# Means of v by band products, their spreads on GpSimd, and a planner that picks one of two engines

## The chip, the cores and the metric

One core of a Trainium2 chip runs the whole program. The metric is the device time of one execution in microseconds; the median of three runs of the kernel before is 602.4 us (602.11 to 602.69).

## What is computed

The reference is attention with a local window and block summaries, then two dense two-layer networks on the 1536 tokens:

```python
B, H, S, D = 2, 8, 768, 64; block, window = 32, 16
k_sum = k.reshape(B, H, S // 32, 32, D).max(axis=3)
v_sum = v.reshape(B, H, S // 32, 32, D).mean(axis=3)
scores_l = where(|i - j| < 16, q @ k.T / 8, -1e9)          # local
scores_s = q @ k_sum.T / 8 + log(32)                       # 24 summaries
a = softmax(concat([scores_l, scores_s]))
x = (a @ concat([v, v_sum])).reshape(1536, 512)
h = x @ w_in;   x = (max(h, 0) + alpha * min(h, 0)) @ w_out     # 512 -> 2048 -> 512
h = x @ w_in2;  y = (h * sigmoid(h)) @ w_out2
```

## The kernel before

Heads go in pairs (4 a batch), queries in 6 blocks of 256 tokens (3 a batch). A pair's keys lie in SBUF as windows of 24 summaries and 160 keys, its values (tile vs, 120 partitions by 12 windows by 128) as 24 means and 96 neighbours; the even windows have the means in partitions 0 to 23, the odd ones in 96 to 119. A group (one block of one pair) passes through these steps: scores (line 554, PE), mask and maximum (L566, L577, DVE), exponentials (L584, ACT), sum and reciprocal (L593, L594, DVE), normalisation (L600, GpSimd), transposes (L606, PE), their copy to pT (L611, ACT), the values (L622, PE), and x as a high and a low half in the rounded float32 format that PE takes fast (L633 ACT, L637 DVE). The four pairs of batch 0 come first, two blocks of each, then the rest, block by block.

The 24 means of a pair are made thus: vT (the whole v of the pair, transposed, 384 KB) is loaded by `load_vt`, for batch 0 into the first half of y, which is free until then, for batch 1 into a staging buffer; DVE sums each block (`sum_v`, L524); PE transposes the sums into PSUM (`turn_v`, L529); ACT writes them with the factor 1/32 from PSUM into all windows of vs (`spread`, L535, step s0 for the first two windows of each kind, s1 for the other four). The maxima of k are made by DVE (L499) and copied to the other five windows by DVE (`copy_k`, L508).

A matrix product of the networks is three products of halves (`three`, L288 to L290). A weight arrives in 512 KB pieces (`load_next`, L121), is put together by three DVE operations on its bits (L147, L151, L154), rounded by ACT (L160, high) and subtracted by GpSimd or DVE (L163, low). The first three pieces land in y beside vT, the later ones in two staging buffers (`raw`). In the first network's first pass each block goes through products with w_in, an activation in four steps (L342 ACT, L348 DVE, L354 ACT, L357: the low half gl, on GpSimd for these blocks), then products with w_out, whose pairs of banks DVE copies to y (L378).

The order of all this, up to two items past the attention, is not written out: every step has an engine, a cost in us, the steps it must follow, a due time (key) and the buffers that it takes and gives. `plan` (L845) repeats: on each engine, of the first 60 steps in order of due time, those whose predecessors are planned; of these the one that can start first; of all engines the earliest. GpSimd's steps and those DVE steps that are marked with lock do not overlap in the plan. Where PE has a gap in the plan, `fill` (L458) puts small products on zeros (L460), up to FILL_END. Loads all go through SP's queue (step `load`, with a modelled wire of RATE MB/us). The instructions are then issued in the plan's order, and the hardware runs each engine's in that order. After it come the remaining passes from a written list.

Of the kernel before, what the change touches and what calls it, by code (L numbers as in the profile page):

```python
# [18 lines left out]
SUB = 64  # L19
PAD = WINDOW  # L20
WIN = SUB + 2 * PAD
P = 128
# [3 lines left out]
AT_KEYS, AT_SUMS, AT_MEANS, AT_SPREAD = -1.1, 1.64, 2.2, 2.35  # L26
AT_EXPS, AT_NORM, AT_TURN, AT_VALUES = 0.22, 0.3, 1.83, 3.2
AT_IN = 5.3
AT_LATER, ITEM_STEP = 4.14, 0.8
CONV, CONV_STEP = -2.94, 0.88  # L30
CONV2, CONV2_STEP = 14.11, -0.2
BATCH, BATCH_STEP = 6.61, 3.24
NQ = 6
STAGE = 2
AT_SC, AT_MASK, AT_X, AT_ACT, AT_OUT = -0.21, 0.0, 3.3, -0.0, 1.54
# [7 lines left out]
def tile_blocks_attention_mlps(  # L43
# [24 lines left out]
    QB = 256  # L68
    BPB = S // QB
# [19 lines left out]
    y_v = y.rearrange("p a n -> p (a n)")[:, :NPAIR * S].rearrange("p (a n) -> p a n", n=S)  # L89
    y_w = y.rearrange("p a n -> p (a n)")[:, NPAIR * S:].rearrange("p (a n w) -> p a n w", n=512, w=2)  # L90
# [34 lines left out]
    def conv_next(eng):  # L125
# [36 lines left out]
        def low():  # L162
# [155 lines left out]
    def activation(u, i, ni, banks):  # L318
# [37 lines left out]
        def four():  # L356
            (nc.gpsimd if early else nc.vector).tensor_tensor(out=gl, in0=g, in1=gh, op=ALU.subtract)  # L357
# [5 lines left out]
    gpool, ps_o = [], []  # L363

    def out_pair(u, m):

        _, ch, t0, n, _ = u
        ps = ps_mm.tile([P, 512], F32, tag="mm", name="ps").rearrange("p (m n) -> p m n", m=2)
        for j in range(2):
            c = slice((m + j) * P, (m + j + 1) * P)  # L370
            for i in range(CF):
                hi, lo = pieces[0, ch, 1, i]
                three(ps[:, j], (hi[:, c], lo[:, c]), g_t[t0, ch * CF + i, 0], i == 0, i == CF - 1)

        def follow():
            if m == KT - 2 and t0 + n == NTOK:
                through[0] = passes.index((0, ch))
            nc.vector.tensor_copy(out=y[:, m:m + 2, t0:t0 + n], in_=ps)  # L378

        return follow  # L380
# [59 lines left out]
    def convert(eng):  # L440
        r = conv_next(eng)
        if r is not None:
            pending.extend(r)
            load_next()

    NG = NBLK * NPAIR
    with ExitStack() as scope0:
# [14 lines left out]
        cst = kv.tile([P, P + 4 * NC], F32, name="cst", bufs=1)  # L462
        ident = cst[:, 0:P]
        mask = cst[:, P:]
# [12 lines left out]
        def load_vt(b, p):  # L477
            if b == 0:
                t = y_v[:, p]
            else:  # L480
                t = stage.tile([P, 512, 2], F32, name="raw").rearrange("p n w -> p (n w)")[:, :S]
# [24 lines left out]
        def copy_k(b, p):  # L506
            t = kt_t[b, p]
            nc.vector.tensor_copy(  # L508
                out=t[:, 1:, :NB], in_=t[:, 0:1, :NB].to_broadcast([P, NTWO, NB])
            )  # L510

        vr_t, pv_t = {}, {}

        def halve_v(b, p):
            v = vt_t[b, p].rearrange("p (n i) -> p n i", i=BLOCK)
            for w in (BLOCK // 2, BLOCK // 4):
                nc.gpsimd.tensor_tensor(
                    out=v[:, :, :w], in0=v[:, :, :w], in1=v[:, :, w:2 * w], op=ALU.add
                )
# [7 lines left out]
        def turn_v(b, p):  # L527
            pt = ps_mm.tile([P, 512], F32, tag="mm", name="pv")
            nc.tensor.transpose(pt[:NB, :P], vr_t.pop((b, p)), ident)  # L529
            pv_t[b, p] = pt  # L530

        def spread(b, p, s0, s1):
            t, ps = vs_t[b, p], pv_t[b, p]
            for at in (t[:NB, s0:s1], t[WIN:, NTWO + s0:NTWO + s1]):
# [4 lines left out]
                    scale=1.0 / BLOCK,  # L539
# [57 lines left out]
        def normalize(blk, p):  # L597
            e = e_t[blk, p]
            rs = sums.pop((blk, p))
            nc.gpsimd.tensor_tensor(out=e, in0=e, in1=rs.to_broadcast([P, 4, NC]), op=ALU.mult)  # L600
# [8 lines left out]
        def turned(blk, p):  # L609
            t = att.tile([NC, 512], F32, tag="pT", name="pT")  # L610
            nc.scalar.copy(out=t, in_=pt_t.pop((blk, p))[:NC])  # L611
            pT_t[blk, p] = t

        def values(blk, p):
# [3 lines left out]
            for i in range(2):  # L618
                for s in range(2):
                    for h in range(2):  # L620
                        c = (2 * h + i) * P + s * SUB
                        nc.tensor.matmul(  # L622
                            ps[h * D:(h + 1) * D, i * P + s * SUB:i * P + (s + 1) * SUB],
                            s_[:, s * NTWO + 2 * j + i, h * D:(h + 1) * D],
                            t[:, c:c + SUB],
                            start=True,
                            stop=True,
# [57 lines left out]
        steps = []  # L685

        def step(name, engine, cost, after, key, f, *a, take=(), give=(), lock=False, size=0):
            steps.append((key, len(steps), name, engine, cost, after, f, a, take, give, lock, size))

        def load(name, key, f, *a, size, after=(), take=()):  # L690
# [3 lines left out]
                "raw": STAGE, "w": 2, "g": 1, "gh": 3}  # L694
# [3 lines left out]
        for p in range(NPAIR):  # L698
            load(("k", 0, p), -100 + at, load_k, 0, p, size=0.41, take=["k"])
            load(("q", 0, p), -100 + at + 0.1, load_q, 0, p, size=0.13, take=["q"])  # L700
            if p == 0:
                load("cst", -100 + at + 0.2, lambda: nc.sync.dma_start(out=cst, in_=consts), size=0.31)
            load(("vt", 0, p), -100 + at + 0.3, load_vt, 0, p, size=0.39)
# [9 lines left out]
        for k, (blk, p) in enumerate(order):  # L713
# [3 lines left out]
            if b and j == 0:  # L717
# [3 lines left out]
                load(("vt", b, p), t + 1.5, load_vt, b, p, size=0.39, take=["raw"])  # L721

        for b in range(B):
            for p in range(NPAIR):
                k = where[b * BPB, p]
                step(("km", b, p), "DVE", 0.87, [("k", b, p)], k + AT_KEYS, prep_k, b, p)
                step(("K", b, p), "DVE", 0.22, [("km", b, p)], k + AT_KEYS, copy_k, b, p, lock=True)
                step(("vr", b, p), "DVE", 0.87, [("vt", b, p)], k + AT_SUMS, sum_v, b, p, BLOCK,
                     take=["vr"], give=["raw"] * (b > 0))

                step(("pv", b, p), "PE", 0.12, [("vr", b, p), "cst"], k + AT_MEANS, turn_v, b, p,
                     take=["mm"], give=["vr"])
# [4 lines left out]
        for k, (blk, p) in enumerate(order):  # L737
# [11 lines left out]
            step(("e", *g), "POOL", 0.95, [("rs", *g)], k + AT_NORM, normalize, *g, lock=True)  # L749
# [4 lines left out]
            step(("o", *g), "PE", 0.47, [("pT", *g), (f"s{int(j > 0)}", b, p)], k + AT_VALUES, values, *g,  # L754
# [6 lines left out]
        def bits(n):  # L761
            halves[n] = conv_next(nc.gpsimd)

        for n in range(3 * CF):
# [4 lines left out]
            step(("lo", n), "POOL", 1.24, [("hi", n)], t + 0.02, lambda n: halves[n][1](), n,  # L769
                 give=["w"], lock=True)  # L770
# [29 lines left out]
        for blk in range(NBLK):  # L800
# [10 lines left out]
            for i in range(0, CF, 2):  # L811
# [3 lines left out]
                else:  # L815
# [6 lines left out]
                step(("a3", blk, i), "POOL", 1.24, [("a2", blk, i)], t0 + AT_ACT, act, blk, i, 3,  # L822
                     give=["g"], lock=True)
            for m in range(0, KT, 2):
# [4 lines left out]
                step(("oc", blk, m), "DVE", 0.6, [("op", blk, m)] + [("vr", 0, p) for p in range(NPAIR)]  # L829
                     + [("cv", n) for n in range(y_w.shape[1])], t,  # L830
                     lambda blk, m: follows[blk, m](), blk, m, give=["mm"])
# [13 lines left out]
        def plan():  # L845
# [4 lines left out]
            locked, wire, out = 0.0, 0.0, []  # L850
            kind, gaps, until = "ps", [], 0.7
# [6 lines left out]
            while any(left.values()):  # L858
                best = None
                for e, todo in left.items():  # L860
                    found = []
                    for s in todo[:60]:
# [5 lines left out]
                        at = max([free[e], *(end[x] for x in after)])  # L868
                        for r in take:
                            at = max(at, sorted(hold[r])[take.count(r) - 1])  # L870
                        if lock:
                            at = max(at, locked)
# [10 lines left out]
                left[e].remove(s)  # L883
# [60 lines left out]
def _layout(q, k, v, moe_w_in, moe_w_out, moe_alpha, moe2_w_in, moe2_w_out):  # L944
# [31 lines left out]
    for t, first in enumerate((0, P, S - P)):  # L976
# [5 lines left out]
        m[t, SUB:, :WIN] = np.where(ok, 0.0, -1000000000.0)[SUB:]  # L982
    consts = np.concatenate(
        [np.eye(P, dtype=np.float32)] + [m[t] for t in (0, 1, 1, 2)], axis=1
# [31 lines left out]
```

## Time and profile before

| | |
|---|---|
| median of 3 runs | 602.4 us |
| the profiled execution | 601.8 us, its span 600.0 us |
| PE busy | 584.0 us (97%) |
| DVE, ACT, GpSimd busy | 415.9, 256.4, 56.1 us |
| granted TensorE clock, mean | 0.994 of full |
| HBM read, written | 48.82, 3.15 MB |

Busy times are of one execution. A product's end is modelled, and the fillers count as busy, so PE's share says little where fillers run; the windows below tell the stages apart. The attention and the first pass lie in the first 155 us or so.

### The profile page before, as it was taken

Reading aid. Unit: us, or ns where it says so; the run is one execution under the profiler, and the core shown is the slowest. Engines: PE = TensorE matmul, PEld = TensorE weight load, DVE = VectorE, ACT = ScalarE, POOL = GpSimd, SP = SyncE. Lnnn points to the kernel's source line nnn. Section 1 sums busy time; section 2 is a strip of 40 time slices with the busy share of each in tenths; the row PEclk is TensorE's granted clock in tenths of the full one; section 3 lists DMA queues with packets and bytes.
Section 4 is the critical chain, followed back from the end, with each engine's and each line's share of the span. In section 5 each row is a group of like instructions: output and inputs, shape, how many; then the busy total and the mean of one; then the engine's idle time right before and its main releaser. Section 6 shows DMA issues by size and latency. Waiting matters only on the chain.

```text
span 600.0 us, 9132 instructions
## 1 busy us (share of the span) xinstructions
PE 584.0 (97%) x3575; PEld 490.1 (82%) x3575; DVE 415.9 (69%) x752; ACT 256.4 (43%) x584; POOL 56.1 (9%) x53
## 2 busy tenths in 40 slices
PE   7989989999899999999999999999999999999997
PEld 5767879899788888888888888888888888888886
DVE  4799888538895573438896789875962598856322
ACT  4888766634242421322543546544612164215110
POOL 0245545321100000000000000000000000000000
PEclk8999989999999999999999999999999999999999
DMA  8988743002542040004030003141130042200111
GB/s 256 314 269 243 208 160 109 32 1 71 153 129 70 3 138 1 0 1 129 19 105 29 0 8 133 71 157 54 37 105 0 1 140 71 72 1 1 69 72 70
DMA packets 24091, 52.55 MB, mean 88 GB/s; under 512 B 2288, under 2 KB 11760, under 8 KB 24048
## 3 DMA queue, kind: packets, MB, share of 16 engines
q1 hardware_dynamic: 24048, 51.97, 27.7%
q8 instruction: 28, 0.46, 0.3%
q14 instruction: 15, 0.12, 0.1%
HBM read 48.82 MB, written 3.15 MB: 87 GB/s over the span
## 4 chain that ended last, share of the span: by engine, by line
PE 78%; DMA 8%; issue 5%; DVE 5%; POOL 2%; SPq 1%; ACT 0%; POOLq 0%; DVEq 0%
PE ps L289 26%; PE ps L288 26%; PE ps L290 25%; DMA raw<-in_w 3%; DMA y<-in_w 1%; DMA q<-in_qT 1%; DMA kT<-in_kT 1%; DVE w L151 1%; DVE w L154 1%; POOL gl L357 1%; DVE w L147 1%; DMA raw<-in_vT 1%; PE sc L554 1%; PE pt L606 1%; PE o L622 1%
## 5 line engine op out<-in xcount | busy, mean ns | idle before, releaser
L288 PE MATMUL ps<-xh,wl 128*128 128x512 f32 (+1 forms) x352 | 127.9, 363 | 0.4 <-POOL wl L163 0.3
L290 PE MATMUL ps<-xh,wh 128*128 128x512 f32 (+1 forms) x352 | 126.8, 360 | 0.0
L289 PE MATMUL ps<-xl,wh 128*128 128x512 f32 (+1 forms) x352 | 126.7, 360 | 0.0
L289 PE MATMUL ps<-gl,wh 128*128 128x512 f32 (+1 forms) x240 | 83.5, 350 | 1.9 <-POOL gl L357 1.8
L290 PE MATMUL ps<-gh,wh 128*128 128x512 f32 (+1 forms) x240 | 83.2, 349 | 0.0
L288 PE MATMUL ps<-gh,wl 128*128 128x512 f32 (+1 forms) x240 | 81.3, 352 | 0.3
L357 DVE TENSOR_TENSOR gl<-g,gh 128x512 fp32r<-128x512 f32 x84 | 57.6, 688 | 31.4 <-ACT gh L354 31.3
L288 PEld LDWEIGHTS ps<-xh,wl 128*128 128x128 f32 x352 | 66.4, 189 | 11.0 <-POOL wl L163 0.8
L289 PE MATMUL ps<-wl,gh 128*128 128x512 f32 (+1 forms) x196 | 75.4, 385 | 0.0
L290 PE MATMUL ps<-wh,gh 128*128 128x512 f32 (+1 forms) x196 | 74.9, 385 | 0.0
L288 PE MATMUL ps<-wh,gl 128*128 128x512 f32 (+1 forms) x196 | 74.9, 385 | 0.0
L290 PEld LDWEIGHTS ps<-xh,wh 128*128 128x128 f32 x352 | 66.4, 189 | 10.0
L289 PEld LDWEIGHTS ps<-xl,wh 128*128 128x128 f32 x352 | 66.5, 189 | 9.8
L354 ACT CAST gh<-g 128x512 fp32r<-128x512 f32 x96 | 59.3, 621 | 25.5 <-DVE g L348 22.1
L342 ACT ACTIVATE m<-ps 128x512 f32<-128x512 f32 x48 | 28.6, 597 | 90.5 <-PE ps L290 90.5
L160 ACT CAST wh<-w 128x512 fp32r<-128x512 f32 x64 | 39.5, 620 | 53.3 <-DVE w L154 34.4
L414 DVE TENSOR_TENSOR y<-ps,y 128x512 f32<-128x512 f32 x48 | 32.4, 688 | 41.9 <-PE ps L290 41.7
L348 DVE SCALAR_TENSOR_TENSOR g<-m,nal,ps 128x512 f32<-128x512 f32 (+1 forms) x60 | 37.2, 637 | 22.6 <-ACT m L342 22.5
L289 PEld LDWEIGHTS ps<-gl,wh 128*128 128x128 f32 x240 | 46.1, 192 | 8.0 <-POOL gl L357 2.3
L288 PEld LDWEIGHTS ps<-gh,wl 128*128 128x128 f32 x240 | 46.1, 192 | 6.8 <-POOL wl L163 0.3
L290 PEld LDWEIGHTS ps<-gh,wh 128*128 128x128 f32 x240 | 46.2, 192 | 5.6
L584 ACT ACTIVATE e<-t,nm 128x120 f32<-128x120 f32 x96 | 36.8, 385 | 19.1 <-DVE nm L577 18.5
(83 smaller groups left out, 844.5 us busy)
## 6 DMA issues: line engine op xcount, KB each, us to landing
raw<-in_w SPq DMA_DIRECT2D x61, 512.0 KB, 3.6
vs<-in_vw SPq DMA_DIRECT2D x16, 288.0 KB, 6.8
kT<-in_kT SPq DMA_DIRECT2D x8, 480.0 KB, 5.8
q<-in_qT SPq DMA_DIRECT2D x24, 128.0 KB, 4.9
out<-y SPq DMA_DIRECT2D x11, 256.0 KB, 2.0
y<-in_vT SPq DMA_DIRECT2D x4, 384.0 KB, 7.8
y<-in_w SPq DMA_DIRECT2D x3, 512.0 KB, 7.9
raw<-in_vT SPq DMA_DIRECT2D x4, 384.0 KB, 4.4
```

What stands on the lines that cost most here:

```text
L147: nc.vector.tensor_scalar(out=w, in0=high, scalar1=3, scalar2=0x3FFFFFFF, op0=ALU.logical_shift_left, op1=ALU.bitwise_and,)
L151: nc.vector.scalar_tensor_tensor(out=w, in0=high, scalar=0xC0000000, in1=w, op0=ALU.bitwise_and, op1=ALU.bitwise_or)
L160: nc.scalar.copy(out=hi, in_=w)
L288: i = nc.tensor.matmul(ps, all_, bh, start=first, stop=False, skip_group_check=again)
L289: nc.tensor.matmul(ps, ah, bl, start=False, stop=False, skip_group_check=again)
L290: nc.tensor.matmul(ps, ah, bh, start=False, stop=last, skip_group_check=again)
L342: nc.scalar.activation(out=m[:, j * w:(j + 1) * w], in_=ps, func=AF.Relu, scale=-1.0)
L348: nc.vector.scalar_tensor_tensor(out=g[:, at], in0=m[:, at], scalar=nal[:, f + j:f + j + 1], in1=ps[:, j * n % w:j * n % w + n], op0=ALU.m ...
L354: nc.scalar.copy(out=gh, in_=g)
L357: (nc.gpsimd if early else nc.vector).tensor_tensor(out=gl, in0=g, in1=gh, op=ALU.subtract)
L414: nc.vector.tensor_tensor(out=at, in0=src, in1=at, op=ALU.add)
L584: nc.scalar.activation(out=e[:, u, :], in_=t[:, u, :], func=AF.Exp, bias=nm[:, u:u + 1], accum_out=sm[:, u, 0:1],)
```

## The change

Batch 0's means are products of the loaded windows with a constant band (1/32 where a row of the window belongs to a block): 12 products of 24 columns, accumulated in PSUM, in place of one transpose. So batch 0's vT is not loaded and not summed, all of y's six places take weights, and the rows of vs that the means will fill are zeroed by GpSimd ahead. For both batches ACT copies the means once from PSUM to a small tile (mn), and GpSimd or ACT spreads them from there. A step may be given several engines: each is a candidate, and one is put aside where another would end it over BIAS = 0.68 us sooner. With the values given, K's copies go to ACT or GpSimd (DVE no longer), the spreads to GpSimd or ACT, the normalisation stays on GpSimd, pT goes to ACT or DVE, a weight's low half to GpSimd or DVE, the copy to y to DVE or ACT, gl to GpSimd or DVE, and for block 5 to DVE alone. The due times and the wire's rate are new. The parts for `split` are unused, since it is empty.

```diff
-AT_KEYS, AT_SUMS, AT_MEANS, AT_SPREAD = -1.1, 1.64, 2.2, 2.35
+AT_KEYS, AT_SUMS, AT_MEANS, AT_SPREAD = -2.12, 1.55, 1.71, 4.61
...
-W_FIRST, W_STEP, W_AHEAD = -98.6, 0.28, 3.41
-SLACK, RATE = 0.0, 0.33
-FILL_LESS, FILL_SLOW, FILL_END = 0.19, 4.0, 61.17
-AHEAD, AT_NEXT = 2, 0.0
+W_FIRST, W_STEP, W_AHEAD = -98.67, -1.13, 4.28
+SLACK, RATE = 0.0, 0.28
+FILL_LESS, FILL_SLOW, FILL_END = 0.65, 4.0, 85.65
+K_ON, SP_ON, E_ON, T_ON, L_ON, O_ON = 1, 2, 1, 2, 0, 0
+BIAS = 0.68
+AHEAD, AT_NEXT = 2, 3.58
...
+    quick = (5,)
+    pooled = (0, 1)
+    banded, split, zeroed = (0,), (), (0,)
...
-    y_v = y.rearrange("p a n -> p (a n)")[:, :NPAIR * S].rearrange("p (a n) -> p a n", n=S)
-    y_w = y.rearrange("p a n -> p (a n)")[:, NPAIR * S:].rearrange("p (a n w) -> p a n w", n=512, w=2)
+    y_w = y.rearrange("p a n -> p (a n)").rearrange("p (a n w) -> p a n w", n=512, w=2)
...
+    def copy(eng, out, in_):
+        (eng.copy if eng is nc.scalar else eng.tensor_copy)(out=out, in_=in_)
...
+        NBAND = 2 * NB - 4
+        cst = kv.tile([P, P + 4 * NC + 2 * NBAND], F32, name="cst", bufs=1)
...
+        band = cst[:, P + 4 * NC:].rearrange("p (o c) -> p o c", o=2)
...
             vs_t[b, p] = t
+            if b in zeroed:
+                nc.gpsimd.memset(t[:NB, :NTWO], 0.0)
...
         def turn_v(b, p):
             pt = ps_mm.tile([P, 512], F32, tag="mm", name="pv")
-            nc.tensor.transpose(pt[:NB, :P], vr_t.pop((b, p)), ident)
             pv_t[b, p] = pt
+            if b not in banded:
+                nc.tensor.transpose(pt[:NB, :P], vr_t.pop((b, p)), ident)
+                return
+            t = vs_t[b, p]
+            for n in range(NSUB):
+                odd, m = divmod(n, NTWO)
+                rows, at = (WIN if odd else NC), NB - 4 - 4 * m
+                nc.tensor.matmul(
+                    pt[:NB, :P], band[:rows, odd, at:at + NB], t[:rows, n],
+                    start=n == 0, stop=n == NSUB - 1,
+                )
...
+        def mean_copy(b, p):
+            mn_t[b, p] = t = kv.tile([NB, P], F32, tag="mn", name="mn", bufs=2)
+            nc.scalar.activation(
+                out=t, in_=pv_t[b, p][:NB, 0:P], func=AF.Copy, scale=1.0 if b in banded else 1.0 / BLOCK
+            )
+
+        def pool_spread(b, p, s0, s1, eng):
+            t, m = vs_t[b, p], mn_t[b, p]
+            for at in (t[:NB, s0:s1], t[WIN:, NTWO + s0:NTWO + s1]):
+                copy(eng, at, m.unsqueeze(1).to_broadcast([NB, s1 - s0, P]))
...
-                step(("K", b, p), "DVE", 0.22, [("km", b, p)], k + AT_KEYS, copy_k, b, p, lock=True)
+                step(("K", b, p), (("DVE", 0.22, True), ("ACT", 0.2, False), ("POOL", 0.2, True))[K_ON:K_ON + 2], 0, [("km", b, p)], k + AT_KEYS, copy_k, b, p)
...
+                if b in banded:
+                    step(("pv", b, p), "PE", 2.65, [("v", b, p), "cst"], k + AT_MEANS, turn_v, b, p, take=["mm"])
...
+                if b in pooled:
+                    step(("mn", b, p), "ACT", 0.2, [("pv", b, p)], k + AT_MEANS + 0.1, mean_copy, b, p, take=["mn"], give=["mm"])
+                    step(("s0", b, p), (("POOL", 0.6, True), ("ACT", 0.7, False))[:SP_ON], 0, [("mn", b, p), ("v", b, p)], k + AT_MEANS + 0.1, pool_spread, b, p, 0, QB // P)
+                    step(("s1", b, p), (("POOL", 1.0, True), ("ACT", 1.2, False))[:SP_ON], 0, [("s0", b, p)], k + AT_SPREAD, pool_spread, b, p, QB // P, NTWO, give=["mn"])
+                    continue
...
-            step(("pT", *g), "ACT", 0.5, [("pt", *g)], k + AT_TURN, turned, *g,
+            step(("pT", *g), (("ACT", 0.5, False), ("DVE", 0.6, False))[:T_ON], 0, [("pt", *g)], k + AT_TURN, turned, *g,
...
-            step(("lo", n), "POOL", 1.24, [("hi", n)], t + 0.02, lambda n: halves[n][1](), n,
-                 give=["w"], lock=True)
+            step(("lo", n), (("POOL", 1.24, True), ("DVE", 0.6, True))[L_ON:], 0, [("hi", n)], t + 0.02, lambda n, eng: halves[n][1](eng), n,
+                 give=["w"])
...
-                step(("a3", blk, i), "POOL", 1.24, [("a2", blk, i)], t0 + AT_ACT, act, blk, i, 3,
-                     give=["g"], lock=True)
+                step(("a3", blk, i), (("POOL", 1.24, True), ("DVE", 0.6, True))[int(blk in quick):], 0, [("a2", blk, i)], t0 + AT_ACT,
+                     lambda blk, i, eng: acts[blk, i][3](eng), blk, i, give=["g"])
...
-                step(("oc", blk, m), "DVE", 0.6, [("op", blk, m)] + [("vr", 0, p) for p in range(NPAIR)]
+                step(("oc", blk, m), (("DVE", 0.6, False), ("ACT", 0.5, False))[O_ON:O_ON + 2], 0, [("op", blk, m)]
...
+                        at = max(free[e], ready)
+                        if any(
+                            max(free[o], ready) + c + BIAS < at + cost for o, c in other.get(s[1], ()) if o != e
+                        ):
+                            continue
```

## Rows read from the trace of the kernel before

**Rows 1.** Windows: start:end, length, busy us (instructions) by engine, clock, DMA share, GB/s

```profile
5.40:36.00 30.60, 26.10 (x328) 20.18 (x328) 23.61 (x53) 21.83 (x80) 8.56 (x9) 0.94 1.03 302
36.00:79.00 43.00, 40.80 (x514) 34.90 (x512) 38.35 (x85) 35.54 (x120) 20.08 (x18) 1.00 0.78 238
79.00:85.00 6.00, 3.13 (x50) 2.34 (x50) 5.90 (x7) 2.17 (x6) 4.65 (x4) 1.00 0.39 115
85.00:90.00 5.00, 5.00 (x52) 4.77 (x53) 4.28 (x10) 4.94 (x17) 1.60 (x2) 0.66 0.43 134
90.00:150.00 60.00, 59.91 (x629) 55.55 (x628) 39.33 (x82) 31.49 (x97) 18.86 (x17) 1.00 0.17 53
150.00:156.00 6.00, 4.02 (x24) 3.31 (x23) 4.54 (x9) 1.86 (x3) 2.15 (x1) 1.00 0.42 124
156.00:597.00 441.00, 440.96 (x1974) 366.25 (x1972) 298.36 (x504) 157.24 (x265) 0.00 (x0) 1.00 0.19 60
```

**Rows 2.** The same windows for line 460 (fillers) alone: PE, PEld, clock, DMA

```profile
5.40:36.00 30.60, 12.59 (x85) 8.81 (x85) 0.94 1.03 302
36.00:79.00 43.00, 6.16 (x41) 3.68 (x41) 1.00 0.78 238
```

**Rows 3.** Chain of waits in time, up to 100 us: start, us, what

```profile
4.45 7.38 DMA kT<-in_kT
...
11.84 8.64 DMA q<-in_qT
...
20.50 8.96 DMA y<-in_w
...
38.18 4.88 DMA raw<-in_w
...
64.70 6.32 DMA raw<-in_w
```

**Rows 4.** Waits: engine line <- releaser: us in total, times, longest

```profile
PE pv L529 <- DVE y L378: 2.6, 1, 2.6
...
PE ps L289 <- POOL gl L357: 1.8, 1, 1.8
```

**Rows 5.** Timeline of DVE and POOL: start, us, engine, line, operation, tiles

```profile
80.38 1.64 DVE L151 SCALAR_TENSOR_TENSOR w<-raw,w 128x512 uint32<-128x512 uint32 x1
...
81.44 1.71 POOL L357 TENSOR_TENSOR gl<-g,gh 128x512 fp32r<-128x512 f32 x1
...
152.85 2.15 POOL L357 TENSOR_TENSOR gl<-g,gh 128x512 fp32r<-128x512 f32 x1 [4.03 <-ACT gh L354]
```

**Rows 6.** Lines by form: operation, shapes xcount | busy us, mean ns | idle before

```profile
L151 DVE SCALAR_TENSOR_TENSOR w<-raw,w 128x512 uint32<-128x512 uint32 x61 | 42.6, 707 | 0.5
...
L524 DVE TENSOR_REDUCE vr<-y 128x24 f32<-128x768 f32 x4 | 3.8, 947 | 0.7 <-DMA y<-in_vT 0.7
...
L508 DVE COPY kT<-kT 128x144 f32<-128x144 f32 x8 | 2.8, 354 | 0.0
...
L357 DVE TENSOR_TENSOR gl<-g,gh 128x512 fp32r<-128x512 f32 x84 | 57.6, 688 | 31.4 <-ACT gh L354 31.3
...
L622 PE MATMUL o<-pT,vs 120*64 120x64 f32 x384 | 15.7, 227 | 0.7 <-DVE xl L637 0.4 <-ACT pT L611 0.3
...
L529 PE MATMUL pv<-cst,vr 128*24 128x128 f32 x8 | 2.2, 277 | 4.5 <-DVE y L378 2.6 <-DVE vr L524 1.1 <-DVE xl L637 0.7
...
L535 ACT ACTIVATE vs<-pv 24x256 f32<-24x256 f32 x16 | 5.9, 370 | 0.4 <-PE pv L529 0.3
...
L535 ACT ACTIVATE vs<-pv 24x512 f32<-24x512 f32 x16 | 9.3, 584 | 0.1
...
L600 POOL TENSOR_TENSOR e<-e,rs 128x480 f32<-128x480 f32 x24 | 23.7, 989 | 58.6 <-DVE rs L594 45.7 <-ACT wh L160 6.5 <-DVE kT L508 2.6
...
L163 POOL TENSOR_TENSOR wl<-w,wh 128x512 fp32r<-128x512 f32 x12 | 16.0, 1334 | 12.1 <-ACT wh L160 12.1
```

**Rows 7.** DMA issues of the page: xcount, KB each, us to landing

```profile
y<-in_vT SPq DMA_DIRECT2D x4, 384.0 KB, 7.8
```

More of the change, by code (lines that the diff above doesn't have):

```diff
@@ L160, in high, with low @@
             nc.scalar.copy(out=hi, in_=w)
-        def low():
+        def low(eng=nc.vector):
             eng.tensor_tensor(out=lo, in0=w, in1=hi, op=ALU.subtract)
@@ L621, in values @@
                         c = (2 * h + i) * P + s * SUB
+                        rows = WIN if s and b in split else NC
                         nc.tensor.matmul(
                             ps[h * D:(h + 1) * D, i * P + s * SUB:i * P + (s + 1) * SUB],
[L624 to L627, printed above, removed]
+                            s_[:rows, s * NTWO + 2 * j + i, h * D:(h + 1) * D],
+                            t[:rows, c:c + SUB],
+                            start=(i, s) == (0, 0) or b not in split,
+                            stop=b not in split,
+                            skip_group_check=b in split,
+                        )
+            if b in split:
+                e_ = t.rearrange("k (h i s c) -> k h s i c", h=2, i=2, s=2)
+                x_ = ps.rearrange("d (i s c) -> d s i c", i=2, s=2)
+                for s in range(2):
+                    for h in range(2):
+                        nc.tensor.matmul(
+                            x_[h * D:(h + 1) * D, s],
+                            mt_t[b, p][:, s, h * D:(h + 1) * D],
+                            e_[:, h, s],
+                            start=False,
+                            stop=s == 1,
+                            skip_group_check=True,
                         )
@@ L683, in tile_blocks_attention_mlps @@
         where = {g: k for k, g in enumerate(order)}
-        steps = []
+        steps, names = [], []
+        engines = {"DVE": nc.vector, "ACT": nc.scalar, "POOL": nc.gpsimd}
         def step(name, engine, cost, after, key, f, *a, take=(), give=(), lock=False, size=0):
-            steps.append((key, len(steps), name, engine, cost, after, f, a, take, give, lock, size))
+            n = len(names)
+            names.append(name)
+            if isinstance(engine, str):
+                steps.append((key, n, name, engine, cost, after, f, a, take, give, lock, size))
+                return
+            for e, cost, lock in engine:
+                steps.append((key, n, name, e, cost, after, f, (*a, engines[e]), take, give, lock, size))
         def load(name, key, f, *a, size, after=(), take=()):
@@ L720, in tile_blocks_attention_mlps @@
                 load(("v", b, p), t + 1.5, load_v, b, p, size=0.6, take=["v"])
-                load(("vt", b, p), t + 1.5, load_vt, b, p, size=0.39, take=["raw"])
+                if b not in banded:
+                    load(("vt", b, p), t + 1.5, load_vt, b, p, size=0.39, take=["raw"])
         for b in range(B):
@@ L850, in plan @@
             locked, wire, out = 0.0, 0.0, []
+            other = {}
+            for s in steps:
+                other.setdefault(s[1], []).append((s[3], s[4]))
+            other = {n: o for n, o in other.items() if len(o) > 1}
             kind, gaps, until = "ps", [], 0.7
@@ L982, in _layout @@
         m[t, SUB:, :WIN] = np.where(ok, 0.0, -1000000000.0)[SUB:]
+    bands = np.zeros((P, 2, 2 * nb - 4), np.float32)
+    for odd, row in ((0, nb + pad), (1, pad)):
+        for i in range(SUB // BLOCK):
+            at = nb - 4 + 2 * odd + i
+            bands[row + i * BLOCK:row + (i + 1) * BLOCK, odd, at] = 1.0 / BLOCK
     consts = np.concatenate(
-        [np.eye(P, dtype=np.float32)] + [m[t] for t in (0, 1, 1, 2)], axis=1
+        [np.eye(P, dtype=np.float32)] + [m[t] for t in (0, 1, 1, 2)] + [bands.reshape(P, -1)], axis=1
     )
```

107 lines of the change are left out of this document (58 added, 49 removed).

## The prediction, made before the changed kernel was run

> **What bounds the kernel now.** I read the windows first, because the share of busy time is a mean over unlike stages. From 156 us to 597 us TensorE is busy 440.96 of 441 us, and from 90 to 150 us 59.91 of 60 [rows 1]: nothing there can be saved except by fewer matmuls, and the change takes none of them away. What can move lies ahead of 90 us and around 152 us. Between 5.4 and 36 us PE shows 26.10 us busy, but 12.59 of that are the filler products of line 460 on zeros, which only keep the clock up [rows 1, 2]; real work is 13.5 us of 30.6. In the same stretch the DMA share is 1.03 at 302 GB/s. Between 36 and 79 us fillers take 6.16 us and PE is idle for another 2.2 us [rows 1, 2]; DVE is busy 38.35 of 43 us. From 79 to 85 us PE works only 3.13 of 6 us, and in the 5 us after it the granted clock is 0.66, the mean of a time at 2.4 GHz and one at 1.2 [rows 1]. At 150 to 156 us PE works 4.02 of 6.
>
> Then the chain of waits says what ends last there. Its early part is one landing after another: 4.45, 11.84 and 20.50 us, each of 7 to 9 us, for kT, q and a weight [rows 3]; the reader sees that no engine but the load queue sets the pace until 29 us. Later pieces of the chain are weights into the two staging buffers (38.18 and 64.70 us) [rows 3]. The two large holes have their releasers in the table of waits: the transpose of batch 1's means waited 2.6 us for a PSUM bank that DVE's copy to y held, and a second matmul waited 1.8 us for GpSimd's low half gl [rows 4]. The timeline shows why the first was late: DVE's conversion beside GpSimd's subtraction took 1.64 us where its mean is 0.707, and GpSimd's own 1.71 us [rows 5, 6].
>
> **The change, part by part.** The sum is made against the profiled execution, 601.8 us (span 600.0 and 1.8 around it); the median of the runs is 602.4, so 0.6 is added at the end. About 0.2% (1.2 us) is what a measurement of this kernel can tell from no change.
>
> A. Four loads of vT, 384 KB each [rows 7], leave the early queue: 1.57 MB at 302 GB/s [rows 1] is 5.2 us; the constants grow by 88 columns (45 KB), 0.15 us back. The last pair's k stands behind three of the four (3.9 us), its v behind all (5.0 net). The chain there is landings, so the gain is real as far as the engines follow. DVE has room for it: it loses four reductions of 0.947 and four copies of 0.354 of 23.61 us [rows 1, 6], so 18.4 us remain for some 25.6. I take -4.0 us; bounds -5.0 and 0. The order of the loads is also rewritten by new keys; a weight more ahead of the last pair is 512 KB, 1.7 us against this.
>
> B. The hole at 79 to 90 us: 2.9 us idle and 5 x (1 - 0.66) = 1.7 us of clock [rows 1]. The copy to y may now go to ACT, which is busy 2.17 of those 6 us [rows 1], and K's copies leave DVE altogether. But the planner's costs know no slow conversion, and GpSimd gets more work that could slow others. What is late next is the conversion itself. I take half, -2.3 us; bounds -4.6 and 0.
>
> C. Block 5's gl goes to DVE alone: 2.15 us there on GpSimd [rows 5] against 0.688 as DVE's mean [rows 6], 1.46 saved on a path where PE waited 1.8 [rows 4]. DVE is busy 4.54 of 6 us [rows 1], so it may stand in a queue: -1.4 us, bounds -1.8 and 0.
>
> D. PE gains 48 band products and loses four transposes. The trace has no matmul of that shape. The values of line 622, with 64 columns on half of the array's width, take 227 ns each with their latency, but overlap: 15.7 us over 384 of them are 41 ns [rows 6]. For 128 columns, if two of them ran beside one another, that is 164 ns, so 2.0 us a pair. The ends: 41 ns (0.5 us a pair) and the transpose's 277 ns with its latency (3.3 us a pair) [rows 6]. I take 2.0, 7.9 us in all, the row that it is nearest to. It lies in place of fillers: 12.59 us of them up to 36 us [rows 2]. Uncovered is what stands in order ahead of a ready product: half of one pair's, +1.0 us; bounds 0 and +7.9, the whole, if the cover is gone. The Trainium skill, FP8 and Floating Point Precision, TensorE Precision Notes, says that true fp32 goes through the array in four passes; 4 x 128 columns at 2.4 GHz would be 213 ns, an estimate, 2.6 us a pair, and the sum by it would be about 0.3 us longer.
>
> E. The spreads: ACT loses two of 0.370 and two of 0.584, 1.91 us a pair [rows 6], and takes a mean's copy (under 0.370) and perhaps K's. GpSimd takes the copies: 1536 elements a pair, at line 600's 0.989 us for 480 not over 3.2 us, and from below near nothing; batch 0 adds a fill with zeros of 768 elements, not over 1.6. ACT stands on no piece of the chain shown [rows 3], so what it gives back is 0; GpSimd is busy 8.56 of 30.6 and 20.08 of 43 us [rows 1], which covers the copies, at 0; without that cover see the second rival. The first values of a pair wait for the second spread, as they did.
>
> F. Three more weights land in y instead of two staging buffers, so fewer wait for a buffer; the two chain pieces were 4.88 and 6.32 us [rows 3], but the wire was 78% busy then [rows 1]. Up to 8.4 us (6.16 + 2.2) stand free on PE there [rows 1, 2]; DVE is 89% busy and sets the next limit. -1.0 us; bounds -4 and +2. K's copies and pT on either engine: 0, under 0.6 us each, PE has fillers beside them.
>
> Sum: 601.8 - 4.0 - 2.3 - 1.4 + 1.0 - 1.0 = 594.1, with 0.6 for the median 594.7 us.
>
> **The rivals.** *First, DVE takes over the pace.* Loads come earlier, but the groups pass at DVE's speed. For it: 89% in the second stretch. Against it: five us of its work leave. Then A and F give nothing and half of B stays: 602.4 - 1.4 - 2.3 + 1.0 = 599.7.
>
> *Second, slower: GpSimd becomes the bound of a batch-0 pair.* Place: between the means and the values. A pair has two normalisations (0.989), a low half (1.334), and now up to 3.2 of copies and 1.6 of zeros: 8.1 us [rows 6]; with the conversion, which the planner locks against GpSimd at 1.65 us, 9.8. A pair takes 30.6 / 4 = 7.65 us now. It decides once copies and zeros cost over 4.3 us a pair, or 2.7 where the lock counts in full. Price 4 x (8.1 or 9.8 - 7.65) = 1.8 or 8.6 us, the middle 5.2. With C and D's uncovered work kept the time is 602.4 + 5.2 - 1.4 + 1.0 = 607.2 (603.8 and 610.6 at the ends). For it: DVE and GpSimd slowed each other at 80 us [rows 5]. Against it: the planner may give spreads to ACT. The Trainium skill, GPSIMD Engine Reference, Specifications, says that GpSimd shares its SBUF interfaces with VectorE, with contention where DVE has two SBUF inputs; the rows at 80 us agree, 1.64 against 0.707. Its section on engine selection calls one-input work on GpSimd roughly line-rate, which at its 1.2 GHz would make the copies 1.3 us a pair, an estimate; no row here shows a copy on GpSimd, and by it this rival would not decide.
>
> *Third, more than forecast.* All of A, B and C, and 4 us of F: 602.4 - 5.0 - 4.6 - 1.8 - 4 = 587.0.
>
> *Fourth, nothing.* The loads keep their place behind weights, the hole moves elsewhere, gains and the band products cancel: 602.
>
> **How the numbers follow.** Forecast 0.52, first rival 0.17, second 0.16, third 0.10, fourth 0.05. Faster: 0.52 + 0.17 + 0.10 = 0.79; same 0.05; slower 0.16. The range runs from 587.0, the third case, to 604.0, the small end of the second; some 0.13 of the second and 0.04 of the third lie outside. The bounds of the forecast's own terms with the same signs lie within it, except where all of D is uncovered, which the second rival's upper part takes in.
>
> **What would show it.** A: the last of batch 0's kT and vs land 4 to 5 us earlier, and the chain's early landings are shorter; wrong if the share of DMA stays at 1 as long as before. B: no PE hole over 1 us near 75 to 90 us, no granted clock under 1 there. C: gl of the last block on DVE, PE busy near 5.4 of 6 us around it. D: 48 products near 2 us a pair, fewer fillers ahead of 36 us. E: GpSimd's copies under 0.5 us for 256 and 1 us for 512 elements, and no values waiting for them. F: weights' landings off the chain. The prediction is wrong if PE's full stretch starts no earlier than now, or if GpSimd or DVE stands between the means and the values.

## The result, and the profile after

The changed kernel takes 596.73 us, the median of four runs (595.28 to 597.33), beside 602.55 for the kernel before: a ratio (of the means) of 0.9895 [0.987, 0.9921], that is 6.3 us less, with 4.8 to 7.8 as the interval; the medians differ by 5.8. The forecast was 594.7 us in a range of 587 to 604. The profiled execution took 596.82 us, its span 595.0.

The same windows as in [rows 1], and the 5 us after 31 us by themselves behind the first row (columns as there):

```profile
5.40:36.00 30.60, 26.97 (x337) 21.40 (x337) 19.95 (x44) 19.86 (x73) 11.50 (x15) 0.94 0.91 257
...
31.00:36.00 5.00, 5.00 (x66) 3.54 (x65) 2.18 (x6) 3.31 (x10) 3.11 (x4) 0.77 0.30 113
36.00:79.00 43.00, 39.26 (x561) 33.06 (x561) 41.81 (x94) 37.73 (x142) 23.70 (x25) 1.00 0.73 219
79.00:85.00 6.00, 5.33 (x74) 4.60 (x71) 5.86 (x13) 3.25 (x12) 2.88 (x3) 1.00 0.37 79
85.00:90.00 5.00, 5.00 (x65) 4.49 (x64) 4.21 (x10) 4.93 (x21) 3.19 (x4) 1.00 0.49 197
90.00:150.00 60.00, 59.44 (x553) 55.78 (x550) 45.11 (x88) 30.27 (x74) 10.75 (x10) 1.00 0.23 80
150.00:156.00 6.00, 6.00 (x48) 5.78 (x47) 3.38 (x7) 2.40 (x4) 0.00 (x0) 1.00 0.61 178
```

Both holes are gone. From 79 to 85 us PE is busy 5.33 of 6 us (before 3.13), and the 5 us after it have the full clock (before 0.66); from 150 to 156 us it is busy 6.00 of 6 (before 4.02). These three rows account for 2.2 + 1.7 + 2.0 = 5.9 us; the two profiled executions differ by 5.0, so they hold the whole gain, and the rest together shows none. The stretch up to 79 us looks as long as it was, and DVE is now nearly full in its second part: 41.81 of 43 us, before 38.35.

What became of the fillers is in the windows of their line alone, and of the band products' line (L536) alone (PE, PEld, clock, DMA):

```profile
5.40:36.00 30.60, 1.99 (x15) 1.20 (x14) 0.94 0.91 257
36.00:79.00 43.00, 2.62 (x16) 1.16 (x16) 1.00 0.73 219
...
5.40:36.00 30.60, 12.42 (x96) 10.17 (x96) 0.94 0.91 257
```

Ahead of 36 us the fillers fell from 12.59 us [rows 2] to 1.99, and the band products took 12.42 in their place. Other work of PE did not come sooner there: without fillers and band products it is 12.56 us, before 13.51. Up to 79 us it is 49.2, before 48.2, about 1 us more. The chain of waits, the table of waits, the timeline (DVE, then PE) around 28 us and the time to landing of the last pair's v say why:

```profile
2.11 4.60 DMA cst<-in_consts
6.73 8.49 DMA vs<-in_vw
15.24 10.43 DMA y<-in_w
...
28.52 4.04 PE pv L536 x24
...
39.16 4.13 DMA kT<-in_kT
```
```profile
PE pv L536 <- DVE xl L685: 2.5, 1, 2.5
...
PE pt L639 <- POOL e L633: 1.6, 3, 1.0
...
PE o L656 <- ACT vs L370: 0.3, 1, 0.3
```
```profile
25.69 0.43 DVE L151 TENSOR_SCALAR w<-y 128x512 uint32<-128x512 uint32 x1 [1.37 <-DMA y<-in_w]
26.15 0.69 DVE L155 SCALAR_TENSOR_TENSOR w<-y,w 128x512 uint32<-128x512 uint32 x1
26.88 0.69 DVE L158 SCALAR_TENSOR_TENSOR w<-y,w 128x512 uint32<-128x512 uint32 x1
...
28.05 0.41 DVE L685 TENSOR_TENSOR xl<-o,xh 128x256 fp32r<-128x256 f32 x1
...
23.18 2.80 PE L536 MATMUL pv<-vs,cst 120*24 120x128 f32 x24
28.52 4.04 PE L536 MATMUL pv<-vs,cst 120*24 120x128 f32 x24 [2.53 <-DVE xl L685]
```
```profile
DMA to landing us min/median/max: 9.7/9.8/9.8
```

Landings still set the chain up to 25.7 us. Then DVE, which had stood 1.37 us for a weight, converts it (three operations), and only behind them makes the low half xl that gives a PSUM bank back; for that bank the last pair's band products waited 2.5 us. Not all of this is the bank's: the last pair's two loads of v, issued at 17.10 and 17.69 us, landed only at 26.8 and 27.5, so the products could have begun 1.7 us sooner at best. They then took 4.04 us where the pair before took 2.80, the clock having fallen (0.77 from 31 to 36 us), and stand on the chain, not under a filler.

The maxima of k of the last pair start as its kT lands (issued at 17.02 us and landed 8.7 us later before, 14.25 and 8.8 after). That pair of batch 0 starts its maximum at 25.75 us before and 23.09 after, and its second load of v is issued at 23.25 before and 17.69 after (the timelines of DVE and of SP; before, then after):

```profile
25.75 0.95 DVE L499 TENSOR_REDUCE kT<-kT 128x24 f32<-128x768 f32 x1
...
23.25 0.33 SPq L489 DMA_DIRECT2D vs<-in_vw  x1
```
```profile
23.09 0.95 DVE L507 TENSOR_REDUCE kT<-kT 128x24 f32<-128x768 f32 x1 [0.97 <-DMA kT<-in_kT]
...
17.69 0.33 SPq L497 DMA_DIRECT2D vs<-in_vw  x1
```

Issued 5.6 us sooner, that load landed 4.3 us sooner, at 27.5 in place of 31.8. These are single traces. In the six traces whose loads keep the changed order (the change and five experiments below) the last kT landed at 22.7 to 24.9 us, in the four with the old order at 25.7 to 26.8; the means lie 2.3 us apart, those of the last v 3.4.

The new operations, in the lines by form, and the line of all GpSimd's spreads (ns: least, median, most):

```profile
L536 PE MATMUL pv<-vs,cst 96*24 96x128 f32 x48 | 7.1, 308 | 0.0
...
L370 POOL COPY vs<-mn 24x512 f32<-24x512 f32 x8 | 6.0, 754 | 0.8 <-ACT mn L556 0.6
L536 PE MATMUL pv<-vs,cst 120*24 120x128 f32 x48 | 5.9, 274 | 2.9 <-DVE xl L685 2.5 <-DMA vs<-in_vw 0.3
...
L370 POOL COPY vs<-mn 24x256 f32<-24x256 f32 x4 | 1.9, 480 | 2.2 <-ACT mn L556 2.1
...
L370 POOL COPY vs<-mn x12: 386/608/969, 30.1 to 90.3; 24x512 f32<-24x512 f32 x8, 24x256 f32<-24x256 f32 x4
```

So GpSimd made only 12 of the 32 copies that spread the means in the changed kernel, the first at 30.1 us; the others went to ACT.

### The profile page after: what moved, and what is told of

Same layout as the page of the kernel before. It is cut to its first block, busy times and chain, and to the rows that moved or that the text cites. A ratio compares the mean times of both kernels' runs of the same rounds, so it can differ in the third digit from the quotient of the medians.

```text
span 595.0 us, 9142 instructions
## 1 busy us (share of the span) xinstructions
PE 582.1 (98%) x3571; PEld 489.1 (82%) x3571; DVE 413.9 (70%) x748; ACT 255.6 (43%) x587; POOL 54.3 (9%) x62
## 4 chain that ended last, share of the span: by engine, by line
PE 87%; DVE 6%; DMA 5%; issue 1%; SPq 0%; ACT 0%; DVEq 0%
PE ps L292 28%; PE ps L293 28%; PE ps L294 28%; DMA y<-in_w 2%; DMA vs<-in_vw 1%; DVE nm L610 1%; PE o L656 1%; DVE t L599 1%; PE pt L639 1%; DMA cst<-in_consts 1%; DVE w L155 1%; DMA kT<-in_kT 1%; PE sc L587 1%; PE pv L536 1%; DVE g L352 1%
## 5 line engine op out<-in xcount | busy, mean ns | idle before, releaser
L361 DVE TENSOR_TENSOR gl<-g,gh 128x512 fp32r<-128x512 f32 x91 | 62.9, 692 | 34.2 <-ACT gh L358 34.0
L292 PE MATMUL ps<-gh,wl 128*128 128x512 f32 (+1 forms) x240 | 79.8, 348 | 0.6 <-ACT pT L370 0.5
L294 PEld LDWEIGHTS ps<-wh,gh 128*128 128x128 f32 x196 | 36.8, 188 | 7.4
```

The lines of the kernel that those rows point to most:

```text
L292: i = nc.tensor.matmul(ps, all_, bh, start=first, stop=False, skip_group_check=again)
L294: nc.tensor.matmul(ps, ah, bh, start=False, stop=last, skip_group_check=again)
L361: eng.tensor_tensor(out=gl, in0=g, in1=gh, op=ALU.subtract)
```

## The experiments

Gains and losses are given against the kernel before: (1 - ratio) x 602.5 us, since that kernel ran beside each (medians of 602.59 to 603.46 us). The change itself stands at -6.3 on this scale. The interval of one ratio is 1.2 to 1.8 us to either side, so the difference of two is good to some 2 us either way; what a wait did is read from the traces.

**The hole at 80 us alone.** The kernel before, with all copies to y (first pass) on ACT:

```diff
-            nc.vector.tensor_copy(out=y[:, m:m + 2, t0:t0 + n], in_=ps)
+            nc.scalar.copy(out=y[:, m:m + 2, t0:t0 + n], in_=ps)
```

> The kernel before with its order kept; the first pass's copies to y are made by ACT and not by DVE, all twelve. Theory (term B: the hole at 79 to 90 us comes from these copies behind DVE's slow conversion, and the pick of ACT is what closed it): PE's lost time between 79 and 90 us was 5.0 us before and 1.2 in the changed kernel, so 2.5 to 3.8 us less: 599.0 against about 602.8. Rival (the bank comes free sooner, but the conversion beside GpSimd's work holds PE at the next matmul): within 1 us of before.

599.74 us, 0.9947 [0.9926, 0.9968]: -3.2 us. One line of the kernel closes the hole (first row: PE busy 10.21 of 11 us at the full clock, where the kernel before had 8.13 and a clock of 0.66 in the second part [rows 1]) and buys half of what the whole change does. The hole at 152 us stays (second row; behind them the same window of the kernel before):

```profile
79.00:90.00 11.00, 10.21 (x138) 8.97 (x136) 9.89 (x19) 8.32 (x23) 6.30 (x5) 1.00 0.44 139
...
145.00:160.00 15.00, 13.80 (x90) 12.49 (x90) 12.16 (x22) 5.29 (x9) 3.46 (x2) 1.00 0.48 161
```
```profile
145.00:160.00 15.00, 13.02 (x90) 11.89 (x90) 13.01 (x23) 4.81 (x8) 3.44 (x2) 1.00 0.53 170
```

**The same with block 5's gl on DVE:**

```diff
-            (nc.gpsimd if early else nc.vector).tensor_tensor(
+            (nc.gpsimd if early and u != units[5] else nc.vector).tensor_tensor(
```

> The kernel before with its order kept; the copies to y on ACT and block 5's gl on DVE together, no band products, vT loaded as ever. Theory (the whole gain of the change comes from closing these two holes, 3.8 and 2.7 us, and the loads saved and the band products cancel): 596.5 against about 602.8, the changed kernel's own time. Rival (the holes are each worth half, the rest comes from the loads): 599.5 or more.

597.55 us, 0.9922 [0.9896, 0.9948]: -4.7 us, without a band product, a spread on GpSimd or a load saved. From 145 to 160 us PE is busy 15.00 of 15 us, with the copies on ACT alone 13.80:

```profile
79.00:90.00 11.00, 10.01 (x131) 8.92 (x134) 9.86 (x19) 7.91 (x23) 5.84 (x5) 1.00 0.49 150
...
145.00:160.00 15.00, 15.00 (x99) 13.74 (x98) 13.02 (x25) 6.10 (x12) 0.00 (x0) 1.00 0.48 145
```

**gl of block 5 by itself**, in the kernel before (the second diff alone):

> The kernel before with its order kept; only block 5's two low halves gl are subtracted by DVE and not by GpSimd. Theory (term C): the wait of 1.8 us at 153 us shrinks by 1.4: 601.1 against 602.5. Rival (DVE's queue there is full, the wait only changes its name): 602.5.

602.05 us, 0.9993 [0.997, 1.0017]: no gain that can be told. The wait is gone from its trace all the same:

```profile
145.00:160.00 15.00, 14.87 (x108) 13.94 (x107) 13.98 (x26) 4.78 (x9) 0.00 (x0) 1.00 0.31 106
```

PE is busy 14.87 of those 15 us, where the kernel before showed 13.02 in the same window, and its table of waits has no wait for gl any more. The interval takes in -1.8, so the time neither bears out nor refutes the forecast of -1.4 for this step.

**The same step undone in the changed kernel**, its order kept:

```diff
         def four(eng=nc.vector):
+            if u == units[5]:
+                eng = nc.gpsimd
```

> The changed kernel in its own order with one thing back: block 5's low half gl runs on GpSimd again (2.15 us there before, against 0.69 on VectorE). Theory (step C is a real wait on the path that sets the end): a PE hole of 1.3 to 2 us comes back near 150 us, PE busy 13 to 13.7 of the 15 us from 145 to 160 (the changed kernel: 15.00), and the time is 1.4 to 2.7 us longer than the changed kernel's 596.7, so 598.1 to 599.4. Rival (once the low half no longer meets a conversion beside it, GpSimd is fast enough): less than 0.5 us longer, PE still busy over 14.7 of those 15 us.

598.13 us, 0.9925 [0.9899, 0.9952]: -4.5, which is 1.8 us less than the change, though by itself this difference is within its uncertainty of some 2 us. The hole is back (13.79 of 15 us, first fence) and GpSimd's gl is its releaser (second, the waits):

```profile
145.00:160.00 15.00, 13.79 (x91) 12.44 (x90) 12.50 (x21) 6.22 (x11) 3.41 (x2) 1.00 0.43 142
```
```profile
PE ps L293 <- POOL gl L363: 1.2, 1, 1.2
```

**The four loads put back** into the changed kernel, into places of y that are free then, with nobody to read them:

```diff
+            if b in banded:
+                nc.sync.dma_start(out=y.rearrange("p a n -> p (a n)")[:, (NPAIR + p) * S:(NPAIR + p + 1) * S], in_=vT[b, p])
```

> The changed kernel with its order of steps kept; the four vT loads of batch 0 (384 KB each) are issued again ahead of each pair's values, into places of y that no weight needs yet, and read by nobody. Theory (the load queue sets the early pace, term A): 1.57 MB at 285 GB/s is 5.5 us, of which 4 (3 to 5.5) come back: 600.7 against 596.7. Rival (DVE and the order on PE pace the pairs, the loads were hidden): under +1, so 597 to 597.7.

599.85 us, 0.9936 [0.9913, 0.9959]: -3.9, so the loads cost 2.5 us, good to 2.1. In its timeline the last pair's maximum of k starts later than even before, and later than in any trace of the changed order without them:

```profile
27.40 0.95 DVE L509 TENSOR_REDUCE kT<-kT 128x24 f32<-128x768 f32 x1 [1.57 <-DMA kT<-in_kT]
```

**The band products alone**, in the order of the kernel before: no vT and no sums for batch 0, 12 products where a transpose stood, the rows for the means zeroed by GpSimd, everything else as it was.

```diff
+            if b:
+                nc.tensor.transpose(pt[:NB, :P], vr_t.pop((b, p)), ident)
+                return
+            t = vs_t[b, p]
+            for n in range(NSUB):
...
+                nc.tensor.matmul(
+                    pt[:NB, :P], band[:rows, odd, at:at + NB], t[:rows, n],
```

> The kernel before with its own order kept; batch 0's vT is not loaded and not summed, its means are the 12 band products in the transpose's place, ACT spreads as before, three places of y stay with the weights. Theory (terms A and D alone, -4.0 and +1.0): 3 us less than before, 599.5 against 602.5. Rival (the old order waits elsewhere, so the freed wire is not used without new due times): within 1 us of before.

605.46 us, 1.0043 [1.0022, 1.0064]: 2.6 us slower, though the loads are gone. The timelines of PE, this kernel first, then the one before, show a place where PE is later:

```profile
16.82 2.80 PE L543 MATMUL pv<-vs,cst 120*24 120x128 f32 x24
...
20.20 0.69 PE L638 MATMUL o<-pT,vs 120*64 120x64 f32 x16
```
```profile
15.92 0.27 PE L529 MATMUL pv<-cst,vr 128*24 128x128 f32 x1
...
16.67 0.69 PE L622 MATMUL o<-pT,vs 120*64 120x64 f32 x16
```

In an order that reckons 0.12 us for a transpose, the next pair's 2.8 us of products stand ahead of the first pair's values (20.20 in place of 16.67 us). In this order the loads' removal did not pay for the products; that the products ahead of the values are the whole of the loss is argued, not shown.

**The wait at 28 us taken away:** the changed order, with the conversion of the second weight (and its two halves) moved behind x of pair 1.

```diff
+            for what, after in [(('cv', 1), ('x', 0, 1)), (('hi', 1), ('cv', 1)), (('lo', 1), ('hi', 1))]:
```

> The changed kernel with one entry of its order moved: the conversion of weight piece 1 (DVE, then ACT and the low half) goes behind the low half of x of block 0, pair 1. In the trace of after, PE waits 2.5 us at 25.7 us for a PSUM bank that this x holds, since DVE stands before it at a weight that lands at 25.7, and the clock falls to 0.77 for 5 us after. Theory (this wait took 2.5 to 3.6 us of what was forecast): 593.1 to 594.7. Rival (what is late next is the weight itself or the last pair's values, and the wait moves there): 596 to 597.

596.94 us, 0.9901 [0.9871, 0.9931]: no gain. The 2.5 us wait is gone from its table, and the last pair's products run at the full clock (2.78 us); but they now wait for the landing of v (first fence), and other waits have grown, above all the transposes' for the normalisation, 1.6 us before the move:

```profile
29.13 2.78 PE L536 MATMUL pv<-vs,cst 120*24 120x128 f32 x24 [0.46 <-DMA vs<-in_vw]
```
```profile
PE pt L639 <- POOL e L633: 4.4, 6, 1.3
```

In this execution that v was issued later, at 19.91 us in place of 17.10, with the order of the loads unchanged. So the two traces are no match line by line; the medians are, and they show no gain.

**Fewer band products:** 2 of 12 a pair, in the changed order. It leaves out 20 of batch 0's 24 means.

```diff
-            for n in range(NSUB):
+            for n in (0, NSUB - 1):
```

> The changed kernel with its order kept; of the 12 band products of each pair of batch 0 only the first and the last are made, so the means of batch 0 leave out 20 of 24 blocks. In after a pair's products take 24 instructions at 0.109 us, 2.6 us; ten of twelve gone are 8.7 us of PE work over four pairs. Theory (the products are mostly uncovered, term D is about +4 and not +1): 592.5 to 594 against 596.7. Rival (they lie in place of fillers and waits for loads, D at most +1): 595.7 to 596.7.

597.99 us, 0.9931 [0.9905, 0.9957]: no gain from some 8.7 us less work on PE. The windows show that the granted clock fell (the third figure from the end of a row):

```profile
5.40:31.00 25.60, 19.31 (x210) 13.83 (x214) 18.12 (x38) 16.52 (x64) 8.40 (x11) 0.74 1.05 285
31.00:36.00 5.00, 4.58 (x57) 3.45 (x49) 2.82 (x7) 3.61 (x11) 3.12 (x4) 0.50 0.31 106
36.00:40.00 4.00, 4.00 (x52) 3.63 (x52) 3.12 (x8) 2.77 (x13) 0.86 (x1) 0.71 0.48 166
```

With PE idle for a quarter of the time up to 31 us the clock stood at its lower level, 1.2 GHz, from 31 to 36 us (0.50), and for part of the time on either side of it; the changed kernel had 0.98, 0.77 and 1.00 in these windows. From 31 to 40 us that alone is 5 x 0.27 + 4 x 0.29 = 2.5 us of full-speed time, about one pair's products, and ahead of 31 us another 25.6 x 0.24 = 6.1, though PE was idle for a part of that. So the test does not give the price of the products on the path: less work and the slower clock cannot be told apart in it. It does show that in the changed kernel the products kept the clock up where the fillers had.

**All spreads on ACT, and all on GpSimd**, each in the changed order (`eng = nc.scalar` or `eng = nc.gpsimd` as the first line of `pool_spread`):

> The changed kernel with its order kept; all spreads of the means are made by ACT, none by GpSimd. Theory (term E: what ACT gives back to GpSimd is worth 0): within 1 us of 596.7. Rival (GpSimd's share is worth something since ACT is 92% busy from 36 to 79 us in this order): 598 or more.

> The changed kernel in its own order with all sixteen first and all sixteen second spreads on GpSimd, none on ScalarE. Theory (step E: GpSimd is covered): the time stays within 1 us of the changed kernel's 596.7; GpSimd has some 5 us more to do over both batches (a copy of 512 took 754 ns there and one of 256 480 ns) of a load that was 11.5 of 30.6 and 23.7 of 43 us. The prediction's second rival (GpSimd becomes the bound of a pair): 1.8 to 8.6 us longer, 598.5 to 605.3, with a wait of the values for a spread over 1 us in the table of waits. With all spreads on ScalarE the time was 597.8.

597.82 us, 0.993 [0.9903, 0.9958], and 598.24 us, 0.9922 [0.9901, 0.9943]: 2.1 and 1.6 us behind the change by the ratios (1.1 and 1.5 by the medians), neither clear of none. With all on GpSimd the values' longest wait for a spread is still short; the normalisation, on the same engine, is waited for more than in the change (1.6 us in all):

```profile
PE pt L640 <- POOL e L634: 3.6, 5, 1.0
...
PE o L657 <- POOL vs L370: 0.3, 1, 0.3
```

That wait is no measure of the copies, however: with all spreads on ACT it came to 3.0 us, and to 4.4 where the conversion was moved.

**Three places in y for weights in place of six.** The order cannot be kept, since a load would then stand in SP's queue for a staging buffer that only a later step frees; so it was planned anew with the changed kernel's due times.

```diff
+        PLACES = 3
...
-                 take=["raw"] * (n >= y_w.shape[1]))
+                 take=["raw"] * (n >= PLACES))
```

> The changed kernel planned anew with three places for weights in y in place of six; the later pieces go to the two staging buffers, as before the change. Theory (step F, six places are worth about 1 us): about 597.7, with weights' landings back in the chain of waits between 36 and 79 us. Upper bound of the prediction for F: 4 us, 600.7. Rival (VectorE, 97% busy from 36 to 79 us, sets that stretch, not the weights): within 0.7 us of 596.7, and VectorE just as full there.

606.41 us, 1.0049 [1.0024, 1.0074]: 9.3 us behind the change, more than either theory's bound. The chain of its profiled run has the landings in it (first fence), and PE has a new hole of 3.1 us ahead of 103.69 us, while DVE makes two conversions in a row (timelines of PE and DVE):

```profile
39.85 5.68 DMA raw<-in_w
...
53.25 8.68 DMA raw<-in_w
```
```profile
103.69 0.58 PE L292 MATMUL ps<-gh,wl 128*128 128x256 f32 x1 [3.14 <-DVE xl L685]
...
99.97 1.52 DVE L151 TENSOR_SCALAR w<-raw 128x512 uint32<-128x512 uint32 x2
101.41 1.28 DVE L155 SCALAR_TENSOR_TENSOR w<-raw,w 128x512 uint32<-128x512 uint32 x2
```

**A new plan with nothing else changed**, one cost brought nearer to what the trace shows. Meant to beat the change:

```diff
-            step(("cv", n), "DVE", 1.65, [("W", n)] + [("cv", n - 1)] * (n > 0), t, bits, n,
+            step(("cv", n), "DVE", 1.85, [("W", n)] + [("cv", n - 1)] * (n > 0), t, bits, n,
```

> The changed kernel planned anew with one cost corrected: the three conversion steps of a weight are planned at 1.85 us in place of 1.65; from 36 to 79 us they took 0.42 + 0.77 + 0.77 = 1.95. Theory (waits left ahead of 79 us come from VectorE running later than planned): 0.7 to 2 us faster than the changed kernel, 594.7 to 596. Rival (VectorE's sum of work sets the pace, so a truer plan only moves the waits): within 0.7 us of 596.7; a new order can also lose up to 2 us, which would show as waits of other products of the same sum.

600.33 us, 0.9976 [0.9956, 0.9996]: 4.9 us behind the change, a miss for theory and rival alike. In its trace PE is busy 9.69 of the 11 us from 79 to 90 us and 53.69 of 55 from 90 to 145, in the changed kernel 10.34 and 54.44. Of twelve experiments none is faster than it.

## Why the prediction was right, and where its terms were off

The direction, the range and the two holes held; the sum was 2 us too good. That it came so near is in part luck: A was taken higher than it measured and B lower, and D's work was mis-sized without a price that could be measured. By its steps:

**A, the four loads, forecast -4.0, bounds -5 and 0.** Real, at -2.5 by the loads put back; with 2.1 us of uncertainty this alone does not exclude -4.0. The traces say that it was sized too high: the landings came sooner by 2.3 us for the last kT and 3.4 for the last v, as means of the traces of either order, not by 4 to 5. The forecast reckoned the saved bytes at the wire's rate of before; up to 31 us the queue moved 285 GB/s in place of 309, why is not shown. And the gain was to be real "as far as the engines follow", with DVE having room: DVE lost the sums, but after the landing the last pair waits for a PSUM bank behind a conversion and then for its own 4.04 us of products. Taking the one wait away brought nothing, so no single wait there has been shown to be the cause; the chain has several of about equal length.

**B, the hole at 79 to 90 us, forecast -2.3, bounds -4.6 and 0.** Right in place and cause: -3.2 by the copies on ACT alone, good to 1.3. Halving it for what might be late next was too cautious by the trace: the conversion that was to be late next cost little, since with the copies on ACT PE is busy 10.21 of the 11 us at the full clock, before 8.13 with 1.7 us of clock lost.

**C, block 5's gl, forecast -1.4.** -1.5 as the difference of the two kernels with and without it beside the copies on ACT, -1.8 as undone in the change, nothing measurable by itself. Each of the three traces shows the wait go with the edit, by 1.2 to 1.9 us of PE's busy time; the time agrees within its intervals, no closer.

**D, the band products, forecast 7.9 us of work, +1.0 of it uncovered.** The work was mis-sized, by a misreading that can be seen in [rows 6]: the trace writes a float32 product as two instructions, so the 384 instructions of line 622 are 192 products (8 in each of 24 groups), and one of them cost 82 ns, not 41; what was scaled up from there had no base. The 24 instructions of a pair took 2.80 us; less the last one's latency of 0.27 that is 2.53 / 23 = 0.110 us from start to start, 0.22 us a product where the prediction took 0.164. Four pairs are 10.6 us at the full clock. The Trainium skill, FP8 and Floating Point Precision, TensorE Precision Notes, was the better guide: the estimate from its four passes was 0.213 us, and the trace agrees with 0.22. That the work lies in the fillers' place held (10.6 us of them went ahead of 36 us); what did not lie there is the last pair's, which stands on the chain. Its price in time stays open, since leaving products out also took the clock away.

**E, the spreads, forecast 0.** GpSimd's copies took 480 and 754 ns in the mean, within the limits given, and the values waited 0.3 us at most in PE's table. But the planner left most of the spreads on ACT, so the change itself tests this step little; the two experiments do. Both ends, all on ACT and all on GpSimd, came out 1 to 2 us behind the planner's mix, within what the comparisons can tell from none. The Trainium skill, GPSIMD Engine Reference, Engine selection, calls one-input work roughly line-rate, and the estimate from it was 1.3 us a pair; the rows make 2 x 0.480 + 2 x 0.754 = 2.5 us, so the trace does not agree. The Trainium skill, GPSIMD Engine Reference, Elementwise — side-by-side cycle accounting, gives 768 ns for 512 elements as the best case: the mean of 754 here lies near it, but copies of 512 took from 0.60 to 0.97 us, so as a best case it does not hold here.

**F, six places in y, forecast -1.0, bounds -4 and +2.** Not settled. The sign held: from 36 to 79 us the changed kernel's chain has one landing, of kT at 39.16, and none of a weight. With three places the time was 9.3 us longer, with the weights' landings in the chain as the theory has it and a hole behind two conversions; but a new plan by itself, with no place taken away, cost 4.9. What the places are worth apart from an order made for them was not measured.

Of the rivals, the first (DVE takes over the pace) came true in its condition, 97% busy from 36 to 79 us, but not in its price: A was not nothing and B was whole, and the time is 3 us under its 599.7. The second (GpSimd) did not come about: with every spread on it GpSimd was busy 28.79 of 43 us and the values waited 0.3 us for a spread, and the time rose by 1.6 us, which is not clear of none and so does not exclude the low end of the rival's price, 1.8. The third needed all of A, B and C and 4 us of F; A fell short, and the time is 9.7 us over its 587.0. The fourth falls with the ratio's interval.

The parts measured one by one, -2.5, -3.2 and about -1.6, make -7.3 against -6.3 measured; that leaves +1.0 for D, E, F and the new order together, with an uncertainty of some 3 us. The forecast had 0 for them. What it had no term for is the order itself: the band products in an order not made for them lost 2.6 us, and one cost in the planner changed by 0.2 us lost 4.9.

## What to carry to other kernels

Ask of each stretch which PE hole has a named releaser before asking how much work is saved: two picks of an engine for a late copy and a late low half brought 4.7 us, while 1.57 MB less to load with 10 us of new products for it, and all the rest, added 1.6, which is within the error. A change that makes a step longer in a planned order has to be measured with a new plan and in the old one; the difference between two plans can be larger than the change. A filler's room is only free as long as the new work does not stand on the chain at the end of it.

## What was not expected of the hardware

A float32 product of 128 columns shows as two instructions of 0.110 us from start to start at the full clock. Where work was taken out of PE with no filler in its place, the clock fell: PE was busy 19.31 of 25.60 us there, at a clock of 0.74 in the mean, and 5 us at 1.2 GHz followed. And the same early loads do not land at the same time in every run: the constants, issued at 2.1 us behind the same loads, took 4.60 us in the changed kernel's profile and 5.54 in that of the spreads on GpSimd, whose queue up to there is the same; the chain of landings shifts with it, and the last kT of batch 0 landed at 23.1 us in the one and 24.4 in the other. How much of the scatter of the times comes from that is not shown.

```profile
2.12 5.54 DMA cst<-in_consts
```
